# Three of a seven's six sums made in the accumulator banks, with a new order of products and of the attention stage

## The chip, the core and the metric

The kernel runs on one core of one Trainium2 chip. The metric is the device time of one execution in microseconds (us); lower is better. TensorE (PE) does the matmuls, VectorE (DVE), ScalarE (ACT) and GpSimd (POOL) the elementwise work, SyncE (SP) issues most of the DMAs. PE writes its results into eight accumulator banks, called `ps` in the rows, that DVE and ACT read.

## What is computed

```python
def _attn_ref(q, k, v):            # 4 batches x 8 heads x 576 positions x 64
    scores = np.matmul(q, k.transpose(0, 1, 3, 2)) / np.sqrt(D)
    scores = np.where(block_i >= block_j, scores, -1e9)   # causal in blocks of 64
    attn = softmax(scores)
    return np.matmul(attn, v)
def _moe_ref(x, w_in, w_out, s, b):    # x 2304 x 512, w_in 512 x 2048, w_out 2048 x 512
    r = np.maximum(x @ w_in, 0.0)
    return (s * (r * r) + b) @ w_out
def _moe2_ref(x, w1, w2, w3, w_out):   # w1, w2, w3 512 x 768, w_out 768 x 512
    return np.maximum(np.maximum(x @ w1, x @ w2), x @ w3) @ w_out
# reference: attention, heads joined to 2304 x 512, then _moe_ref, then _moe2_ref
```

All of it is in float32. The kernel splits each operand into a high and a low half and makes three matmuls of each product (high by high, high by low, low by high).

## The kernel before

**Attention** takes sixteen pairs of heads, one after the other. For a pair PE makes the scores of nine units of up to 576 columns, DVE takes each unit's maximum (L516), ACT the exponential with the row sums (L520, an ACTIVATE and a short read of its accumulator), PE turns the results by transposes (L581), ACT copies the turned tiles from the banks to SBUF (L363, `other<-ps`), and PE multiplies them by the values. ACT also copies the pair's result into the array `xf` (L363, `xf<-ps`). While a pair is worked on, the next pair's keys and queries are split: POOL takes high halves (L359), DVE low halves (L368, 64x1152), and ACT or POOL two small tiles of 64x128 called `k0`. A weight that layer 1 needs is read by DMA as words of 64 bits and converted by DVE, ACT, DVE, DVE (L704, L708, L712, L716), then split into halves. Three such weights are prepared from the twelfth pair on (`pre`).

**Layer 1, first half of its hidden units**: five chunks of tokens, eight blocks of 128 hidden units each (40 steps), with plain products of 128x512 or 128x384. Beside it DVE and ACT prepare the weights of what follows ("aside") and write them to DRAM (`wscr`, `bscr`): for layer 1's second half from step 8 on, for layer 2 from step 24 on in every other step, and then one in each seven of layer 1.

**Layer 1, second half, and layer 2's first three products** are made by "sevens": a product of 2x2 blocks by seven block products instead of eight (39 sevens: 12 in layer 1, 27 in layer 2). The seven products are named after the weight blocks: A11, S1, S2, S3, A12, S4, A22. Each is six matmuls of 128x384 into one bank. Four results C11, C12, C21, C22 come from seven products by sums. In the kernel before, each product has a bank of its own. ACT copies the first (L914), and DVE makes six sums in each seven (L902), each of a bank and an SBUF tile. In layer 1 ACT then makes relu, square and affine of the four results (`hidden`, L1232, L1237, L1244). In layer 2 DVE takes the maximum over the three weights (L1303). The blocks are fetched from `bscr` by `next_b`, seven for each seven, into a ring of eight places. Between the products of a seven stand the products with the second weight (`l2_half`, `l4`) of the seven before.

**What sets the order.** The functions only record operations with their reads and writes. `Sched.run` (L200) then goes through them with a cost for each engine and a latency for each pair of engines: at each step the engine that is free first takes the operation that is ready and stands earliest in the record, shifted by its kind's entry in `CFG["off"]`. An operation that may run on two engines takes the one that gets to it first (`CFG["pe"]`, `CFG["je"]`, `CFG["eng"]`). The order in which an engine gets its instructions is fixed when the program is built; on the chip an instruction whose input is late holds up all behind it on its engine. Banks are given out by `Banks.get`, the one that was taken longest ago first. A seven has four banks, the accumulators of the second product the other four.

Of the kernel before, what the change touches and what calls it, by code (L numbers as in the profile page):

```python
# [46 lines left out]
ABLK = ("A11", "S1", "S2", "S3", "A12", "S4", "A22")  # L47
BBLK = ("B11", "T1", "T2", "T3", "B21", "B22", "T4")
# [23 lines left out]
def c_act(n):  # L72
    return n / 1.2 + 51
# [199 lines left out]
def tile_attention_moe(ctx: ExitStack, tc: tile.TileContext, qk, vp, w_in, w_out, s_, b_, w123, w_out2, out):  # L273
# [96 lines left out]
    def mm(o, l, r, start, stop):  # L370
        nc.tensor.matmul(o, l, r, start=start, stop=stop)  # L371
# [376 lines left out]
    def prepare_b(key, kind):  # L748

        G, G2 = (convert(src, kind) for src in wsrc[key])  # L750
# [134 lines left out]
    def product(A, B, where):  # L885

        W, bank = wuse.pop(A), banks.get(where)
        o = bank.ap[:, 0:HN]
        for i in range(2):
            X = xs[B, i]  # L890

            def f(e, i=i, X=X):
                kk = slice(128 * i, 128 * i + 128)
                mm(o, W.ap[:, 0, kk], X.ap[:, 0, :], i == 0, False)
                mm(o, W.ap[:, 0, kk], X.ap[:, 1, :], False, False)
                mm(o, W.ap[:, 1, kk], X.ap[:, 0, :], False, i == 1)
            op("PE", 3 * c_mm(HN), f, reads=[(W, 0), (W, 1), (X, 0), (X, 1)], writes=[bank], kind="l1")
        return bank
# [5 lines left out]

    def seven(key, P1, dst, between):


        m1, u2, u3, u4 = (rings["u"].get() for _ in range(4))
        for a in ABLK:
            wuse[a] = ready.pop(key + (a,))  # L910
        M = product("A11", "B11", P1)

        def f(e, M=M):
            nc.scalar.activation(out=m1.ap, in_=M.ap[:, 0:HN], func=AF.Copy)  # L914
        op("ACT", c_act(HN), f, reads=[M], writes=[m1], kind="u")
# [4 lines left out]
        c = {"C22": dst("C22")}  # L920
        add_to(c["C22"], M5, u3)
        for _ in range(4):
            next_b()
        between()
        for x, a, b, u in (("C11", "A12", "B21", m1), ("C12", "S4", "B22", u4), ("C21", "A22", "T4", u3)):
            M = product(a, b, P1)
            c[x] = dst(x)
            add_to(c[x], M, u)
            next_b()
        return c  # L930
# [200 lines left out]
    def prepare_aside(todo_, kind):  # L1131
        if todo_:
            key = todo_.pop(0)
            (prepare_v if isinstance(key[0], str) else prepare_b)(key, kind)
# [73 lines left out]
    for i, (n_, f_) in enumerate(steps):  # L1208
        s_now, c = PASSES[n_]
        while direct and (("in", min(i + 2, HF - 1)) not in ready or i + 2 >= LAG and ("out", min(i + 2 - LAG, HF - 1)) not in ready):  # L1210
            prepare_direct("w")
        l1(c, f_, banks.get(SETS[0]))
# [223 lines left out]
```

## Time and profile before

| | |
|---|---|
| median of 3 runs | 845.12 us (844.29 to 845.18) |
| profiled execution | 843.48 us |
| its span, first to last instruction | 841.7 us |
| PE busy | 826.4 us (98%) |
| DVE busy | 644.5 us (77%) |
| ACT busy | 466.7 us (55%) |
| POOL busy | 47.5 us (6%) |
| mean granted TensorE clock | 0.997 of full speed |

Busy is the time in which an engine had at least one instruction under way. Matmuls overlap in their pipeline, so a busy PE is not always at its full rate; the count of matmuls in a stretch shows the rate. A group of rows below gives an instruction's line, engine, operation, output and input tile, shape, count, busy time and mean duration, then the idle time of its engine before it and who ended that.

### The profile page before, as it was taken

The page shows a single profiled execution, that of the slowest core. Times are in us where ns is not written, and L with a number is a line of the kernel's source. Part 1 is how long each engine was busy: PE and PEld are TensorE (multiplying, and loading weights), DVE is VectorE, ACT ScalarE, POOL GpSimd, SP SyncE. Part 2 cuts the span into 40 slices and gives each one's busy share as a digit, 9 for nine tenths or more (in the row PEclk, how much of TensorE's full clock was granted, in tenths as well). Part 3 has the DMA queues.
Part 4 walks back from the last instruction along what each step waited for, and adds up shares of the span by engine and source line. Part 5 has one row for each costly group of instructions (what it writes and reads, how often), then busy time and mean ns, then how long its engine had stood idle before and what let it go on. Part 6 is the DMA issues. An engine that isn't in the chain of part 4 may idle for free.

```text
span 841.7 us, 14337 instructions
## 1 busy us (share of the span) xinstructions
PE 826.4 (98%) x4922; PEld 749.0 (89%) x4922; DVE 644.5 (77%) x1329; ACT 466.7 (55%) x1077; POOL 47.5 (6%) x65
## 2 busy tenths in 40 slices
PE   8999999999999999999999999999999999999997
PEld 7777777778888889998999999999998999999996
DVE  7778889999879697895997865857569466937762
ACT  5889999998668577666857726721014111411112
POOL 6222222100000000000000000000000000000000
PEclk9999999999999999999999999999999999999999
DMA  7669777766878787999659526557665676557742
GB/s 278 178 197 267 211 238 238 226 209 205 307 264 292 262 282 281 332 367 365 218 186 365 167 96 210 154 182 251 203 206 162 219 219 213 175 178 229 230 126 76
DMA packets 86088, 190.82 MB, mean 227 GB/s; under 512 B 10240, under 2 KB 16640, under 8 KB 86016
## 3 DMA queue, kind: packets, MB, share of 16 engines
q1 hardware_dynamic: 85456, 189.38, 68.6%
q8 instruction: 39, 0.64, 0.3%
q10 hardware_dynamic: 560, 0.52, 0.2%
q14 instruction: 33, 0.27, 0.1%
HBM read 145.49 MB, written 40.71 MB: 221 GB/s over the span
## 4 chain that ended last, share of the span: by engine, by line
PE 74%; DVE 9%; DMA 7%; ACT 6%; issue 3%; POOL 0%; SPq 0%; ACTq 0%; DVEq 0%; POOLq 0%
PE ps L371 70%; DMA bscr<-other 5%; PE ps L581 4%; ACT other L520 2%; DVE other L716 2%; DVE arena L368 2%; ACT other L363 2%; DVE other L368 1%; DVE other L764 1%; DVE other L704 1%; DMA arena<-bscr 1%; DMA pscr<-other 1%; ACT other L708 1%; DVE other L712 1%; DMA arena<-arena 1%
## 5 line engine op out<-in xcount | busy, mean ns | idle before, releaser
L371 PE MATMUL ps<-arena 128*128 128x384 f32 (+6 forms) x3878 | 736.7, 348 | 5.5 <-ACT other L363 1.4
L371 PEld LDWEIGHTS ps<-arena 128*128 128x128 f32 (+1 forms) x3878 | 677.1, 189 | 59.2 <-ACT other L520 9.5
L902 DVE TENSOR_TENSOR other<-ps,other 128x384 f32<-128x384 f32 x273 | 145.9, 553 | 81.1 <-PE ps L371 77.9
L368 DVE TENSOR_TENSOR arena<-other,arena 128x384 fp32r<-128x384 f32 (+3 forms) x204 | 136.3, 682 | 20.7 <-ACT arena L355 17.7
L355 ACT ACTIVATE arena<-other 128x384 fp32r<-128x384 f32 (+3 forms) x124 | 66.1, 545 | 113.9 <-DVE other L1303 68.0
L363 ACT ACTIVATE other<-ps 128x512 f32<-128x512 f32 (+1 forms) x137 | 72.1, 581 | 33.3 <-PE ps L371 23.9
L516 DVE TENSOR_REDUCE other<-ps 128x1 f32<-128x448 f32 (+4 forms) x144 | 68.8, 513 | 21.1 <-PE ps L371 17.6
L520 ACT ACTIVATE other<-ps,other 128x448 f32<-128x448 f32 (+4 forms) x144 | 79.3, 564 | 9.1 <-DVE other L516 8.1
L914 ACT ACTIVATE other<-ps 128x384 f32<-128x384 f32 x39 | 19.1, 489 | 109.8 <-PE ps L371 89.4
L581 PE MATMUL ps<-ident,other 128*128 128x128 f32 x400 | 55.8, 280 | 4.4 <-ACT other L520 3.8
L371 PE MATMUL ps<-other 128*64 128x64 f32 (+5 forms) x640 | 54.9, 313 | 0.1
L355 ACT ACTIVATE other<-other 128x256 fp32r<-128x256 f32 (+2 forms) x87 | 37.0, 437 | 27.7 <-DMA bscr<-other 14.1
L368 DVE TENSOR_TENSOR other<-other 128x256 fp32r<-128x256 f32 (+1 forms) x105 | 46.0, 453 | 8.0 <-ACT other L355 7.4
L581 PEld LDWEIGHTS ps<-ident,other 128*128 128x128 f32 x400 | 45.0, 143 | 8.0 <-ACT other L520 5.2
L708 ACT ACTIVATE other<-other 128x512 f32<-128x512 f32 x56 | 38.2, 694 | 20.8 <-DVE other L704 20.7
L371 PEld LDWEIGHTS ps<-other 128*64 128x64 f32 (+1 forms) x640 | 29.7, 136 | 19.3 <-issue 14.3
L716 DVE SCALAR_TENSOR_TENSOR other<-other 128x512 uint32<-128x512 uint32 x56 | 38.3, 688 | 3.9 <-ACT other L708 2.9
L1232 ACT ACTIVATE other<-other 128x384 f32<-128x384 f32 x48 | 24.6, 517 | 29.2 <-DVE other L902 29.2
L1303 DVE TENSOR_TENSOR other<-other 128x384 f32<-128x384 f32 x72 | 38.7, 554 | 1.3
L359 POOL TENSOR_SCALAR arena<-other 128x1152 fp32r<-128x1152 f32 (+4 forms) x31 | 33.7, 1102 | 53.3 <-PE ps L371 42.6
L357 DVE TENSOR_SCALAR arena<-other 128x384 fp32r<-128x384 f32 (+2 forms) x73 | 27.8, 384 | 10.9 <-ACT other L962 6.9
L1244 ACT ACTIVATE other<-other,cst 128x384 f32<-128x384 f32 x48 | 32.7, 699 | 0.4
(38 smaller groups left out, 383.9 us busy)
## 6 DMA issues: line engine op xcount, KB each, us to landing
arena<-bscr SPq DMA_DIRECT2D x273, 256.0 KB, 3.1
bscr<-other SPq DMA_DIRECT2D x91, 256.0 KB, 3.7
other<-qk SPq DMA_DIRECT2D x30, 576.0 KB, 6.4
other<-w_out SPq DMA_DIRECT2D x22, 512.0 KB, 6.0
other<-w SPq DMA_DIRECT2D x18, 512.0 KB, 5.4
other<-vp SPq DMA_DIRECT2D x16, 544.0 KB, 5.0
other<-w_in SPq DMA_DIRECT2D x16, 512.0 KB, 4.2
wscr<-other SPq DMA_DIRECT2D x14, 512.0 KB, 5.8
```

Of the source, the lines that this page charges most:

```text
L355: nc.scalar.activation(out=dst, in_=src, func=AF.Copy, scale=m)
L359: nc.gpsimd.tensor_scalar(out=dst, in0=src, scalar1=m, scalar2=1.0, op0=ALU.mult, op1=ALU.mult)
L363: nc.scalar.activation(out=dst, in_=src, func=AF.Copy)
L368: eng[e].tensor_tensor(out=dst, in0=a, in1=b, op=ALU.subtract)
L371: nc.tensor.matmul(o, l, r, start=start, stop=stop)
L516: nc.vector.tensor_reduce(out=NM.ap[:, u:u + 1], in_=v, axis=AX.X if n <= 512 else AX.XY, op=ALU.max, negate=True)
L520: nc.scalar.activation(out=ev, in_=v, func=AF.Exp, bias=NM.ap[:, u:u + 1], scale=1.0, accum_out=DEN.ap[:, d:d + 1])
L581: nc.tensor.transpose(TB.ap[:, 128 * i:128 * i + 128], x, ident)
L708: nc.scalar.activation(out=hi_f, in_=hi_f, func=AF.Prelu, scale=W_REBIAS, alpha=W_SIGN)
L716: nc.vector.scalar_tensor_tensor(out=lo_w, in0=hi_w, scalar=3, in1=lo_w, op0=ALU.logical_shift_left, op1=ALU.bitwise_or)
L902: nc.vector.tensor_tensor(out=out_.ap, in0=bank.ap[:, 0:HN], in1=u.ap, op=ALU.add)
L1303: eng[e].tensor_tensor(out=u.ap, in0=c.ap, in1=u.ap, op=ALU.max)
```

## The change

The sums that need one operand in a bank are made by PE where it can: after ACT has copied a bank out, a later product is accumulated on it. For that the order of the seven products changes to A11, S1, A12, S2, S4, S3, A22. A11 and S1 open banks a and b. A12 opens a third, d. S2 is added on bank a after ACT has copied it (`m1`), S4 on bank b after ACT has copied that (`m5`), S3 on bank a after ACT has copied it again (`u2`). A22 is added on bank a after DVE has read it for C22, and the bank then holds C21, which nobody copies by itself: ACT's relu reads it in layer 1, DVE's maximum in layer 2. So a seven has three copies by ACT (line 907 of the changed kernel) and three sums by DVE (line 902) in place of one and six. Bank a now stays taken from the first product of a seven to the last.

```diff
-ABLK = ("A11", "S1", "S2", "S3", "A12", "S4", "A22")
-BBLK = ("B11", "T1", "T2", "T3", "B21", "B22", "T4")
+ABLK = ("A11", "S1", "A12", "S2", "S4", "S3", "A22")
+BBLK = ("B11", "T1", "B21", "T2", "B22", "T3", "T4")
...
-    def product(A, B, where):
-        W, bank = wuse.pop(A), banks.get(where)
+    def product(A, B, bank, start=True):
+        W = wuse.pop(A)
...
-                mm(o, W.ap[:, 0, kk], X.ap[:, 0, :], i == 0, False)
+                on = dict(skip_group_check=not start)
+                mm(o, W.ap[:, 0, kk], X.ap[:, 0, :], start and i == 0, False, **on)
...
+    def out_of(bank, u, func=AF.Copy, kind="u"):
+        def f(e):
+            nc.scalar.activation(out=u.ap, in_=bank.ap[:, 0:HN], func=func)
...
     def seven(key, P1, dst, between):
-        M = product("A11", "B11", P1)
-            nc.scalar.activation(out=m1.ap, in_=M.ap[:, 0:HN], func=AF.Copy)
-        M5 = product("S1", "T1", P1)
-        add_to(u2, product("S2", "T2", P1), m1)
-        add_to(u4, M5, u2)
-        add_to(u3, product("S3", "T3", P1), u2)
-        add_to(c["C22"], M5, u3)
...
+        a = banks.get(P1)
+        product("A11", "B11", a)
+        m1 = out_of(a, rings["u"].get())
+        b = banks.get(P1)
+        product("S1", "T1", b)
+        m5 = out_of(b, rings["u"].get())
+        d = banks.get(P1)
+        product("A12", "B21", d)
+        add_to(c["C11"], d, m1)
+        product("S2", "T2", a, False)
+        u2 = out_of(a, rings["u"].get())
+        product("S4", "B22", b, False)
+        add_to(c["C12"], b, u2)
+        product("S3", "T3", a, False)
+        add_to(c["C22"], a, m5)
         between()
+        product("A22", "T4", a, False)
+        c["C21"] = a
...
-            prepare_aside(aside, "w2")
-        if i >= CFG["aside2"] and i % 2:
-            prepare_aside(aside2, "w2")
+            prepare_aside(aside, "w2", gate)
+        if i in CFG["aside2"]:
+            prepare_aside(aside2, "w2", gate)
...
-CFG = {'aside': 8, 'aside2': 24,
+CFG = {'aside': 8,
+        'aside2': (16, 18, 20, 22, 24, 26, 28, 30),
...
-        'je': ['ACT'],
+        'je': ['ACT', 'DVE'],
...
-        'pe': ['ACT'],
+        'pe': ['ACT', 'DVE'],
...
-        'pre': (0, 0, 0, 0, 0, 0, 0, 0, 0, 0, 0, 1, 1, 1),
+        'pre': (0, 0, 0, 0, 0, 0, 0, 0, 1, 0, 0, 0, 0, 0, 0, 1, 0),
```

Five more things change. The copies of the turned tiles and of the results into `xf` may go to DVE as well as to ACT. The `k0` tiles of pairs after the second go to POOL alone, and of the low halves POOL may take some. The record's order inside a pair (`CFG["order"]`) and nearly all of the shifts in `CFG["off"]` are other numbers. Two weights of layer 1 are prepared during attention, at the ninth and the sixteenth pair, instead of three from the twelfth on. The eight preparations for layer 2 that stood in steps 25 to 39 stand in steps 16 to 30, and a preparation's loads now wait for the first product of their step or seven (`gate`).

On PE, where two sevens of layer 2 meet, every six matmuls are a block product. `Activation` and `DVE` are those engines' semaphores, the DMA names those of the block's fetch. Before, these are S3, A12, A22, S4 of one seven and A11 of the next:

```order
L371 MATMUL ps<-arena 128x384 [waits DMAHW5_49]
L371 MATMUL ps<-arena 128x384 x5
L371 MATMUL ps<-arena 128x384 [waits DMAHW6_49,Activation_49]
L371 MATMUL ps<-arena 128x384 x5
L371 MATMUL ps<-arena 128x384 [waits DMAHW1_49,DVE_49]
L371 MATMUL ps<-arena 128x384 x5
L371 MATMUL ps<-arena 128x384 [waits DMAHW7_49,DVE_49]
L371 MATMUL ps<-arena 128x384 x5
L371 MATMUL ps<-arena 128x384 [waits DMAHW0_49]
L371 MATMUL ps<-arena 128x384 x5
```

Now, at the same place, A12, S1, S2, S4 and S3 of one seven, in this order on PE:

```order
L371 MATMUL ps<-arena 128x384 [waits DMAHW4_49]
L371 MATMUL ps<-arena 128x384 x5
L371 MATMUL ps<-arena 128x384 [waits DMAHW1_49,DVE_49]
L371 MATMUL ps<-arena 128x384 x5
L371 MATMUL ps<-arena 128x384 [waits DMAHW3_49,Activation_49]
L371 MATMUL ps<-arena 128x384 x5
L371 MATMUL ps<-arena 128x384 [waits DMAHW5_49,Activation_49]
L371 MATMUL ps<-arena 128x384 x5
L371 MATMUL ps<-arena 128x384 [waits DMAHW6_49,Activation_49]
L371 MATMUL ps<-arena 128x384 x5
```

S1 waits until DVE has read the bank of the seven before, and S2, S4 and S3 each wait for a copy by ACT. Between the product whose bank is copied or read and the product that waits, there is one other product (six matmuls) here for S1, S4 and S3.

On ACT, in a middle pair of attention, before:

```order
L520 ACTIVATE other<-ps,other 128x448
L355 ACTIVATE other<-other 64x128
L520 ACTIVATE other<-ps,other 128x64
L363 ACTIVATE other<-ps 128x384
L520 ACTIVATE other<-ps,other 128x192
L363 ACTIVATE other<-ps 128x512
L520 ACTIVATE other<-ps,other 128x448
L520 ACTIVATE other<-ps,other 128x576
L520 ACTIVATE other<-ps,other 128x320
L363 ACTIVATE xf<-ps 128x64
L363 ACTIVATE xf<-ps 128x512
```

and now:

```order
L520 ACTIVATE other<-ps,other 128x192
L363 ACTIVATE other<-ps 128x512
L520 ACTIVATE other<-ps,other 128x64
L363 ACTIVATE other<-ps 128x384
L355 ACTIVATE arena<-xf 128x512
L363 ACTIVATE other<-ps 128x512
L520 ACTIVATE other<-ps,other 128x576
L363 ACTIVATE xf<-ps 128x64
L520 ACTIVATE other<-ps,other 128x448
L520 ACTIVATE other<-ps,other 128x320
L363 ACTIVATE other<-ps 128x384
```

The `k0` tile (64x128) is gone from ACT, and no large copy into `xf` stands between these exponentials; the exponentials are the same ones in another order.

## Rows read from the trace of the kernel before

**Rows 1.** Engines by stretch: start:end, length, busy (count) by engine, clock, DMA share, GB/s.

```profile
24.40:155.70 131.30, 127.88 (x1111) 96.60 (x1110) 110.46 (x170) 121.17 (x374) 33.05 (x40) 1.00 0.77 227
155.70:176.50 20.80, 19.54 (x189) 14.55 (x187) 18.77 (x42) 20.62 (x58) 0.00 (x0) 1.00 0.57 181
176.50:300.00 123.50, 123.50 (x551) 102.31 (x548) 109.11 (x254) 90.05 (x162) 0.00 (x0) 1.00 0.75 258
300.00:325.00 25.00, 24.53 (x128) 22.35 (x126) 22.37 (x56) 18.31 (x36) 0.00 (x0) 1.00 0.90 336
...
375.00:400.00 25.00, 23.16 (x131) 22.27 (x130) 14.40 (x30) 14.17 (x29) 0.00 (x0) 1.00 0.99 371
400.00:550.00 150.00, 150.00 (x866) 149.69 (x865) 122.58 (x280) 99.58 (x207) 0.00 (x0) 1.00 0.61 199
550.00:825.00 275.00, 275.00 (x1498) 263.71 (x1497) 181.80 (x359) 50.35 (x100) 0.00 (x0) 1.00 0.62 197
...
sum 841.70, PE 826.41 PEld 748.95 DVE 644.52 ACT 466.71 POOL 47.48; mean PE 82.64 PEld 74.90 DVE 64.45 ACT 46.67 POOL 4.75
```

**Rows 2.** Chain that ended last: the same seven transposes, thirteen pairs apart (start, length).

```profile
24.45 0.77 PE ps L581 x7
...
155.70 0.78 PE ps L581 x7
```

**Rows 3.** Engines by stretch, as Rows 1: two single pairs of attention.

```profile
85.95:95.39 9.44, 9.44 (x87) 7.41 (x86) 8.43 (x12) 9.00 (x29) 2.88 (x3) 1.00 0.59 194
95.39:106.21 10.82, 10.23 (x89) 7.39 (x87) 9.05 (x17) 9.93 (x34) 2.45 (x3) 1.00 0.78 225
```

**Rows 4.** Groups of instructions by shape, 0 to 176.5 us (attention): ACT, DVE and POOL.

```profile
L363 ACT ACTIVATE other<-ps 128x512 f32<-128x512 f32 x64 | 39.1, 631 | 2.4 <-PE ps L581 2.4
...
L363 ACT ACTIVATE other<-ps 128x384 f32<-128x384 f32 x48 | 23.9, 519 | 4.0 <-PE ps L581 3.9
...
L363 ACT ACTIVATE xf<-ps 128x512 f32<-128x512 f32 x15 | 9.3, 622 | 0.0
...
L355 ACT ACTIVATE other<-other 64x128 f32<-64x128 f32 x16 | 4.9, 309 | 0.4 <-DMA other<-qk 0.4
...
L363 ACT ACTIVATE xf<-ps 128x64 f32<-128x64 f32 x15 | 3.5, 237 | 0.0
...
L368 DVE TENSOR_TENSOR arena<-other,arena 64x1152 fp32r<-64x1152 f32 x14 | 28.6, 2045 | 1.5 <-POOL arena L359 1.3
...
L359 POOL TENSOR_SCALAR other<-other 64x128 f32<-64x128 f32 x16 | 4.8, 301 | 48.5 <-DVE other L516 21.0 <-PE ps L371 11.6 <-issue 8.8
```

**Rows 5.** Groups by shape, whole run: sums and weight conversion, DVE's copies, ACT's copy.

```profile
L902 DVE TENSOR_TENSOR other<-ps,other 128x384 f32<-128x384 f32 x273 | 145.9, 553 | 81.1 <-PE ps L371 77.9
...
L716 DVE SCALAR_TENSOR_TENSOR other<-other 128x512 uint32<-128x512 uint32 x56 | 38.3, 688 | 3.9 <-ACT other L708 2.9
L712 DVE TENSOR_SCALAR other<-other 128x512 uint32<-128x512 uint32 x56 | 23.5, 421 | 0.0
L704 DVE TENSOR_SCALAR other<-other 128x512 f32<-128x512 f32 x56 | 23.4, 420 | 2.7 <-DMA other<-w 2.2 <-DMA other<-w_out 0.5
...
L365 DVE COPY other<-ps 128x512 f32<-128x512 f32 x9 | 6.1, 683 | 14.5 <-DMA out<-other 14.5
...
L914 ACT ACTIVATE other<-ps 128x384 f32<-128x384 f32 x39 | 19.1, 489 | 109.8 <-PE ps L371 89.4 <-DVE other L902 20.4
```

**Rows 6.** Timeline at 383 to 388 us, DVE and PE (start, length, idle before and releaser).

```profile
383.72 0.36 DVE L357 TENSOR_SCALAR arena<-other 128x384 fp32r<-128x384 f32 x1 [0.46 <-ACT other L1244]
...
384.14 2.27 PE L371 MATMUL ps<-arena 128*128 128x384 f32 x9 [0.42 <-DVE arena L357]
...
387.67 2.54 PE L371 MATMUL ps<-arena 128*128 128x384 f32 x13 [1.27 <-DMA arena<-bscr]
```

**Rows 7.** Chain that ended last, at the end: from PE's last matmul to ACT.

```profile
799.94 35.29 PE ps L371 x179
...
835.30 0.61 ACT other L363
```

**Rows 8.** Groups by shape, 400 to 825 us: PE's matmuls of the sevens.

```profile
L371 PE MATMUL ps<-arena 128*128 128x384 f32 x2088 | 365.2, 334 | 0.0
```

More of the change, by code (lines that the diff above doesn't have):

```diff
@@ L368, in sub_to, with mm @@
         eng[e].tensor_tensor(out=dst, in0=a, in1=b, op=ALU.subtract)
-    def mm(o, l, r, start, stop):
-        nc.tensor.matmul(o, l, r, start=start, stop=stop)
+    def mm(o, l, r, start, stop, **k):
+        nc.tensor.matmul(o, l, r, start=start, stop=stop, **k)
     def load(size, f, eng="SP", after=(), lat=2000, **k):
@@ L746, in prepare_v, with prepare_b @@
         pair_out("wv", G.ap[..., 0], [(G, "lo")], 512, wscr[VAT_[key]], key, kind)
-    def prepare_b(key, kind):
-        G, G2 = (convert(src, kind) for src in wsrc[key])
+    def prepare_b(key, kind, after=()):
+        G, G2 = (convert(src, kind, after) for src in wsrc[key])
         half = slice(0, 256), slice(256, 512)
@@ L1129, in prepare_direct, with prepare_aside @@
             ready[key] = prepare_v(key, kind, key[0][0] + "w%d" % key[1], after)
-    def prepare_aside(todo_, kind):
+    def prepare_aside(todo_, kind, after=()):
         if todo_:
             key = todo_.pop(0)
-            (prepare_v if isinstance(key[0], str) else prepare_b)(key, kind)
+            (prepare_v if isinstance(key[0], str) else prepare_b)(key, kind, after=after)
     def next_b():
@@ L1228, in tile_attention_moe, with hidden @@
         ready["out", f_] = fetch("oc%d" % i, ("out", f_), kind="wf")
-    def hidden(u):
+    def hidden(u, bank=None):
         def f(e):
             nc.scalar.activation(out=u.ap, in_=u.ap, func=AF.Relu)
-        op("ACT", c_acts(HN), f, reads=[u], writes=[u], kind="h", lock=True)
+        if bank:
+            out_of(bank, u, AF.Relu, "h")
+        else:
+            op("ACT", c_acts(HN), f, reads=[u], writes=[u], kind="h", lock=True)
         def f(e):
@@ L1259, in dst @@
                 return rings["rc" if x[2] == "1" else "kp"].get()
+            gate = [len(sch.ops)]
             c = seven((i, "in"), P1, dst, between)
             f1, f2 = HF + i, HF + i + HF // 2
-            for x in ("C11", "C21", "C22", "C12"):
-                hidden(c[x])
+            bank, c["C21"] = c["C21"], dst("C21")
+            for x in ("C11", "C12", "C22", "C21"):
+                hidden(c[x], bank if x == "C21" else None)
             split_h((f1, 0), c["C11"])
@@ L1300, in tile_attention_moe, with f @@
                 c = seven((i, w), P1, dst, between)
-                for x in ("C22", "C11", "C12", "C21") if w else ():
-                    def f(e, u=best[x], c=c[x]):
-                        eng[e].tensor_tensor(out=u.ap, in0=c.ap, in1=u.ap, op=ALU.max)
-                    op(CFG_E("max", DVE=c_dve(HN), Pool=c_pooltt(HN)), 0, f, reads=[c[x], best[x]], writes=[best[x]], kind="h", lock=True)
+                if not w:
+                    out_of(c["C21"], dst("C21"))
+                for x in ("C11", "C12", "C22", "C21") if w else ():
+                    v = c[x].ap[:, 0:HN]
+                    def f(e, u=best[x], v=v):
+                        eng[e].tensor_tensor(out=u.ap, in0=v, in1=u.ap, op=ALU.max)
+                    op("DVE", c_dve(HN), f, reads=[c[x], best[x]], writes=[best[x]], kind="h", lock=x != "C21")
             split_h((i, 0), best["C11"])
@@ L1334 @@
                'hlo': ['DVE'],
-               'max': ['DVE'],
                'whi': ['ACT', 'DVE'],
@@ L1362 @@
                 'u': -200,
-                'w0': 250,
+                'w0': -975,
                 'w2': 100,
@@ L1376 @@
         'q0': ['ACT', 'SP'],
+        'q2d': 2,
         'raw': 4,
@@ L1380 @@
         'warm': 60,
-        'xs': 12}
+        'xs': 16}
 def kernel(**inputs):
```

58 lines of the change are left out of this document (28 added, 30 removed).

## The prediction

> **What bounds the kernel now.** I read the table of engines by stretch first, then the chain that ended last, then the groups by shape in attention, then the few places where PE waits after attention. The table [rows 1] has two regimes. From 176.5 us on PE is busy all the time but for 0.47 us in 300 to 325, 1.84 us in 375 to 400, and the tail. The counts say that this is the full rate: 866 matmuls of 384 columns in 150 us is 0.173 us each, the same wherever PE is full. The change leaves the number and the shapes of PE's matmuls as they are, so in that part it can win back only those stalls, however much it takes off DVE. In 550 to 825 us, DVE is busy 181.8 of 275 us and ACT 50.4, beside a full PE.
>
> Before 176.5 us it is different. In 24.4 to 155.7 us ACT is busy 121.2 of 131.3 us (92%), DVE 110.5 (84%), and PE has 3.4 us without any matmul. The chain passes the same seven transposes at 24.45 and 155.70 us, thirteen pairs apart [rows 2]: 131.25 / 13 = 10.10 us for a pair. A pair in which PE never stops takes 9.44 us; a slow one takes 10.82, and there ACT is busy 9.93 and DVE 9.05 us [rows 3]. So a pair has 0.66 us that is not PE's own, on the average, and thirteen have 8.5 us. In the last stretch, 155.7 to 176.5, ACT is the full engine: 20.62 of 20.80 us [rows 1].
>
> **The change, part by part.**
>
> *Attention: work leaves ACT.* Counted in the built order up to the last exponential, ACT loses 5 copies of 128x512 and 9 of 128x384 out of the banks, 8 large and 11 small copies into `xf`, and 14 `k0` tiles: 5 x 0.631 + 9 x 0.519 + 8 x 0.622 + 11 x 0.237 + 14 x 0.309 = 19.7 us [rows 4], of some 142 us that it is busy in 24.4 to 176.5. DVE gets the copies. A copy of 128x512 takes it 0.683 us [rows 5]; at ACT's durations for the rest that is about 5 x 0.68 + 9 x 0.52 + 8 x 0.68 + 11 x 0.24 = 16.1 us. Three weight conversions fewer begin there, 3 x (0.420 + 0.421 + 0.688) = 4.6 us [rows 5]. Net, DVE has 11.5 us more: its 110.5 + 18.8 us become 141 of 152 us, 93% (some of it falls into the first pair). POOL has 14 tiles of 0.301 us more [rows 4], and is mostly idle. So ACT goes from 93% to (141.8 - 19.7) / 152 = 80%, and DVE comes to stand where ACT stood. PE's order in a pair keeps its form: two blocks of matmuls by the values, and transposes between scores. The most to win is 8.5 us (every pair at 9.44). The other end is a loss: were DVE to set the pairs as ACT does in the slow one, the 11.5 us would come on top. I take half of the 8.5, 4.2 us, since a shorter queue on ACT shortens every exponential's wait while DVE still has its heavy pairs. In the last stretch PE has 1.26 us idle beside a full ACT [rows 1]; I take 1.0. For the first pair, whose splitting is dealt out anew, I take 0, between -1.5 and +1.5. Sum: -5.2 us.
>
> *Shared port.* DVE's subtraction of 64x1152, with both inputs in SBUF, takes 2.045 us [rows 4]; an estimate by its columns from the copy of 128x512 (0.683, [rows 5]) is 1.5. It runs where POOL works on the next pair's high halves. The Trainium skill (SBUF — State Buffer, "SBUF: two separate sides") gives a reason: a VectorE operation with two SBUF inputs and a GpSimd operation share a port pair that one holds for its whole instruction while the other blocks. The trace agrees in kind. By that rule the 14 added tiles on POOL could hold DVE up 14 x 0.301 = 4.2 us at most. The sum would be 841.5 by it if all of that stood on PE's path, between the forecast and the third rival; without it the sum stands as it is.
>
> *Sevens: sums move from DVE to PE's banks.* DVE loses 156 sums of 0.553 us (86 us), ACT gets 78 copies of 0.489 us and nine more for layer 2's first results [rows 5]. On a full PE that is worth 0 by itself. It costs where a copy is late. Now three products in each seven wait for a copy or a read, and in the built order 96 waits (66 on ACT, 30 on DVE) have one other product between the product that fills the bank and the one that waits. That product is 6 x 0.173 = 1.04 us. Against it stand: the last matmul's record runs 0.334 us [rows 8], 0.16 beyond its slot; 0.07 from PE's end to ACT's start (835.23 to 835.30) [rows 7]; the copy, 0.49, or the sum, 0.55; and 0.06 back to PE (384.08 to 384.14) [rows 6]. Together 0.78 on ACT and 0.84 on DVE, so 0.26 and 0.20 us are left. In layer 2 ACT is busy 50 of 275 us and the copy meets an empty queue: 0. In layer 1 ACT is at 66% [rows 1], and its queue holds relu, square and affine of 0.5 to 0.7 us. A copy that finds one just begun is late by up to 0.7 - 0.26 = 0.44 us, and PE and the products behind it wait. Ends: 0, and 12 sevens x 3 x 0.44 = 15.8 us. I take 1.0, near the lower end, as the order was laid out so that most copies find ACT free.
>
> *Preparations for layer 2 come earlier.* In 375 to 400 us PE makes 131 matmuls, 144.5 at its full rate (25 / 0.173): 2.3 us lost. One part is 1.27 us for a block from `bscr` while the DMA engines are 99% busy [rows 1, 6]; another is a split by DVE that waited for ACT's affine, 0.42 us [rows 6]. Eight preparations, each two loads of 512 KB (one for an output weight) with its conversions and up to seven stores of 256 KB through SP's queue, go from steps 25 to 39 to steps 16 to 30, some 45 us earlier, where no block is fetched yet. DMA was at 75% there, so the stores fit, and SP's queue is freer when the sevens start fetching. I take 2.0 of the 2.3 us; ends 0 and 2.8 (with the 0.47 in 300 to 325).
>
> *Layer 1's weights start later.* Three conversions that were done in attention fall into its first steps: with the low halves' subtraction, at about 0.69, 3 x 2.2 = 6.6 us of DVE, and each step takes two weights after the third. In the first three steps only one is due, so they hide there; 0, with the other end at 6.6 us. *The tail* has the same last products and stores: 0.
>
> Sum: 843.48 - 5.2 + 1.0 - 2.0 = 837.3 us for an execution like the profiled one. The median of the runs shown lies 845.12 - 843.48 = 1.64 us higher, so I forecast 838.9.
>
> **The rivals.**
>
> First, attention keeps its pairs. The waits before PE's transposes are still for exponentials, which stay on ACT; if that latency, not ACT's load, makes the 0.66 us, nothing is won there. For it: pairs of 10.82 us have ACT idle for 0.9 us. Against it: the fast pairs have less work on ACT and DVE. It gives 838.9 + 5.2 = 844.1.
>
> Second, the other side: copies are late in the sevens of layer 1. The price is up to 15.8 us in place of 1.0, 853.7. The whole gain of 5.2 + 2.0 us is gone when the 36 waits lose 7.2 / 36 = 0.20 us each. For it: there is 0.26 us where the kernel before, counted the same way, left 0.5 us and more; ACT's queue is in order. Against it: the low load in two thirds of the sevens.
>
> Third, DVE takes ACT's place: its load of 93% in attention, its subtractions of 2.045 us beside POOL [rows 4], and the late weights hold back what ACT frees. Then some 5 of the 7.2 us come back: 844. Heavy pairs speak for it (DVE 9.05 of 10.82, [rows 3]), the light ones (8.43 of 9.44) leave 1 us.
>
> **How the numbers follow.** Forecast 0.53, first rival 0.15, second 0.14, third 0.18. The forecast's own range is 833 to 842.5. From these, faster by over 0.2% (1.7 us; about what a measurement tells from no change), below 843.4: nearly all of the forecast and a third of the first and third, 0.64. Within 0.2%: 0.19. Slower: 0.17, most of the second and the ends of the others. For 8 in 10 the range goes from 832 to 848: all of what attention and the stalls could give, less the forecast's own doubt, up to half of the second rival's price.
>
> **What would show it.** In the profile after: a pair near 9.7 us and ACT's busy share in attention near 80%, DVE's over 90%; PE without idle time at 383 to 388 us; matmuls at 0.173 us through layer 2's sevens. Wrong would be: pairs still at 10.1 us; PE idle released by ACT's line 907 in the sevens, by over 0.2 us at a time; fewer than 144 matmuls in 25 us between 400 and 550; PE waiting for weights in the first steps of layer 1.

## The result, and the profile after

The changed kernel takes 834.61 us (median of 4 runs, 833.58 to 835.5) against 845.15 for the kernel before (4 runs, 844.29 to 845.28): a ratio of 0.9871 [0.9854, 0.9889], 10.5 us less. The forecast was 838.9 us, 6.2 less. The profiled execution takes 834.42 us, its span 832.6.

To see where the 9.06 us between the two profiled executions went, I cut both spans at three points that PE passes in either: the first large block by the values of the first pair (first matmul), the same block thirteen pairs later, and the last transposes.

| stretch | before | after | change | forecast |
|---|---|---|---|---|
| start to the first block | 22.32 | 19.12 | -3.20 | 0 |
| thirteen pairs | 131.25 | 127.06 | -4.19 | -4.2 |
| from there to the last transposes | 19.85 | 18.58 | -1.27 | -1.0 |
| last transposes to the end | 668.26 | 667.88 | -0.38 | -1.0 |

The first two rows hide what is steady and what is not. Up to the second pair's large block, eight of the experiments below have the same order of instructions as after, yet that block starts at 29.14 us in after and anywhere from 29.16 to 31.83 us in the eight; in before it starts at 32.52 us. The twelve pairs from there on take 121.05 us in before (120.96 and 121.01 in two experiments with its order) and 117.04 in after (116.78 to 116.90 in seven experiments with its order). So the -4.0 us of these twelve pairs and the -1.27 us of the last stretch are firm, 5.3 us together. The -3.4 us ahead of them are not: of the nine profiles, after's has the earliest start of that block.

Engines by stretch of after (columns as in [rows 1]), the thirteen pairs cut at the transposes that [rows 2] show for before, then the last stretch and three later ones:

```profile
21.04:148.10 127.06, 125.02 (x1113) 97.28 (x1109) 120.34 (x198) 111.78 (x337) 42.84 (x52) 1.00 0.80 231
148.10:168.90 20.80, 20.80 (x205) 16.67 (x202) 20.69 (x47) 19.43 (x52) 0.00 (x0) 1.00 0.61 184
375.00:400.00 25.00, 24.44 (x139) 23.57 (x138) 15.97 (x35) 20.59 (x41) 0.00 (x0) 1.00 1.01 354
400.00:550.00 150.00, 149.37 (x858) 148.34 (x857) 108.95 (x256) 98.32 (x201) 0.00 (x0) 1.00 0.64 212
550.00:825.00 275.00, 275.00 (x1483) 261.57 (x1483) 132.19 (x256) 71.32 (x145) 0.00 (x0) 1.00 0.62 193
```

A pair now takes 127.06 / 13 = 9.77 us in place of 10.10. ACT's share fell from 92 to 88%, DVE's rose from 84 to 95%: DVE is now the fuller engine. In 375 to 400 us PE makes 139 matmuls in place of 131, but in 400 to 550 it makes 858 in place of 866: what was won in the one stall came back in others. 858 in 150 us is 143 in 25 us, just below the 144 that the prediction named as a sign of being wrong. In 550 to 825 DVE has lost 50 us of work, and the end does not move for it.

What PE waits for after attention, in before and then in after (waited for, us, times, longest):

```profile
PE ps L371 <- DMA arena<-bscr: 1.3, 1, 1.3
PE ps L371 <- DVE arena L357: 0.4, 1, 0.4
PE ps L371 <- ACT other L363: 0.4, 1, 0.4
```

```profile
PE ps L371 <- DMA arena<-bscr: 0.9, 2, 0.4
PE ps L371 <- DVE arena L368: 0.9, 1, 0.9
PE ps L371 <- DVE other L902: 0.2, 1, 0.2
```

No wait in after ends on an ACT copy (L907). The 0.9 on L368 is new: at 188 us a weight of layer 1 is prepared late, another of the prediction's signs of being wrong.

Two single pairs of after, one of the two slow ones that are left (the other takes 10.81) and a fast one:

```profile
76.79:87.81 11.02, 10.16 (x87) 7.53 (x86) 10.93 (x19) 9.51 (x29) 4.08 (x4) 1.00 0.87 252
97.46:106.73 9.27, 9.27 (x87) 7.40 (x86) 8.94 (x15) 8.27 (x25) 2.71 (x4) 1.00 0.82 250
```

The fast pair is faster than the 9.44 us that I took for the floor [rows 3]; in the slow one DVE is busy 10.93 of 11.02 us, so it has no time left there.

The first pair, 16 to 20 us, before and then after; the column behind the five engines is the granted clock:

```profile
16.00:18.00 2.00, 1.09 (x5) 0.85 (x6) 1.94 (x4) 1.94 (x8) 1.77 (x3) 0.70 0.79 309
18.00:20.00 2.00, 2.00 (x12) 2.00 (x11) 2.00 (x2) 1.44 (x3) 0.80 (x1) 0.50 0.63 130
```

```profile
16.00:18.00 2.00, 2.00 (x17) 1.93 (x18) 0.46 (x2) 2.00 (x6) 1.52 (x3) 1.00 0.99 361
18.00:20.00 2.00, 2.00 (x12) 1.27 (x13) 2.00 (x4) 0.90 (x4) 2.00 (x2) 1.00 0.70 274
```

The first transposes on PE with the wait ahead of them, before and then after:

```profile
16.43 0.44 PE L581 MATMUL ps<-ident,other 128*128 128x128 f32 x2 [1.28 <-ACT other L520]
```

```profile
15.15 0.44 PE L581 MATMUL ps<-ident,other 128*128 128x128 f32 x2 [1.04 <-ACT other L520]
```

Before has 0.50 of the clock (1.2 GHz) there, after PE had waited 1.28 us ahead of the first transposes; after waits 1.04 us at that place and keeps 2.4 GHz. I had not looked at this stretch.

### The profile page after: what moved, and what is told of

Its sections match the earlier page's. It is cut to its first block, busy times and chain, and to the rows that moved or that the text cites. A ratio compares the mean times of both kernels' runs of the same rounds, so it can differ in the third digit from the quotient of the medians.

```text
span 832.6 us, 14344 instructions
## 1 busy us (share of the span) xinstructions
PE 820.8 (99%) x4922; PEld 747.7 (90%) x4922; DVE 589.7 (71%) x1227; ACT 489.9 (59%) x1097; POOL 57.7 (7%) x78
## 4 chain that ended last, share of the span: by engine, by line
PE 84%; DVE 7%; DMA 6%; issue 1%; ACT 1%; POOL 0%; SPq 0%; DVEq 0%; ACTq 0%; POOLq 0%
PE ps L371 80%; PE ps L581 4%; DVE arena L368 2%; DMA other<-qk 1%; DMA other<-w_in 1%; DMA arena<-bscr 1%; DMA other<-w_out 1%; DVE other L716 1%; DVE other L516 1%; DMA arena<-wscr 1%; DMA bscr<-other 1%; DVE other L368 1%; DVE xf L812 0%; DVE other L712 0%; DVE other L764 0%
## 5 line engine op out<-in xcount | busy, mean ns | idle before, releaser
L371 PE MATMUL ps<-arena 128*128 128x384 f32 (+7 forms) x3878 | 731.1, 347 | 5.3 <-ACT other L520 1.5
L368 DVE TENSOR_TENSOR arena<-other,arena 128x384 fp32r<-128x384 f32 (+3 forms) x205 | 134.0, 665 | 30.3 <-ACT arena L355 25.3
L907 ACT ACTIVATE other<-ps 128x384 f32<-128x384 f32 x138 | 67.6, 490 | 147.6 <-PE ps L371 147.3
L902 DVE TENSOR_TENSOR other<-ps,other 128x384 f32<-128x384 f32 x117 | 64.9, 554 | 97.6 <-PE ps L371 94.6
L355 ACT ACTIVATE arena<-other 128x384 fp32r<-128x384 f32 (+4 forms) x115 | 63.0, 554 | 67.0 <-PE ps L371 54.0
L363 ACT ACTIVATE other<-ps 128x512 f32<-128x512 f32 (+1 forms) x122 | 63.8, 561 | 41.9 <-PE ps L371 30.0
L520 ACT ACTIVATE other<-ps,other 128x576 f32<-128x576 f32 (+4 forms) x144 | 78.2, 555 | 10.1 <-DVE other L516 9.0
L516 DVE TENSOR_REDUCE other<-ps 128x1 f32<-128x576 f32 (+4 forms) x144 | 68.4, 512 | 4.9 <-PE ps L371 3.2
L357 DVE TENSOR_SCALAR arena<-other 128x384 fp32r<-128x384 f32 (+1 forms) x82 | 30.4, 374 | 28.6 <-ACT other L1260 16.1
L368 DVE TENSOR_TENSOR other<-other 128x256 fp32r<-128x256 f32 (+1 forms) x105 | 46.9, 456 | 3.7 <-ACT other L355 3.1
L365 DVE COPY other<-ps 128x512 f32<-128x512 f32 (+2 forms) x29 | 17.6, 620 | 27.4 <-DMA out<-other 26.4
L368 DVE TENSOR_TENSOR arena<-xf,arena 128x384 fp32r<-128x384 f32 (+1 forms) x56 | 32.8, 598 | 1.3 <-ACT arena L355 1.0
```

What stands on the lines that cost most here:

```text
L355: nc.scalar.activation(out=dst, in_=src, func=AF.Copy, scale=m)
L363: nc.scalar.activation(out=dst, in_=src, func=AF.Copy)
L368: eng[e].tensor_tensor(out=dst, in0=a, in1=b, op=ALU.subtract)
L371: nc.tensor.matmul(o, l, r, start=start, stop=stop, **k)
L516: nc.vector.tensor_reduce(out=NM.ap[:, u:u + 1], in_=v, axis=AX.X if n <= 512 else AX.XY, op=ALU.max, negate=True)
L520: nc.scalar.activation(out=ev, in_=v, func=AF.Exp, bias=NM.ap[:, u:u + 1], scale=1.0, accum_out=DEN.ap[:, d:d + 1])
```

## The experiments

### Half of the change at a time

Attention's settings of after in the kernel before, with the sevens and the steps of the preparations as they were:

```diff
-CFG = {'aside': 8, 'aside2': 24, 'eng': {'k0': ['ACT', 'Pool'], ...
+CFG = {'aside': 8, 'aside2': 24, 'eng': {'k0': ['Pool'], ...   # all of after's, but for 'aside2' and 'ew'
```

> The kernel before with the changed kernel's settings of attention alone (record's order, shifts, engines of the splits and copies, when layer 1's weights are prepared); sevens and the preparations for layer 2 as before. Theory A (attention makes the gain; the sevens are worth about nothing on a full PE): the changed kernel is 10.5 us below before, of which its trace has 8.8 us by the start of layer 1, so 835 to 837.5, with the stalls of before at the start of the sevens (some 3 us) kept. Theory B (the lighter DVE in the sevens and the earlier preparations carry half or more of it): 840 or more.

Measured: 848.15 us (846.55 to 850.59), ratio 1.0043 [1.0028, 1.0058]. Attention has after's pace (last transposes at 165.64 us, after 164.76, before 173.42), yet the kernel is slower than before. The rest takes 683.1 us in place of 668.3. Most of it is at one place: PE's rows where layer 1's sevens start, and engines by stretch there:

```profile
384.73 5.12 PE L371 MATMUL ps<-arena 128*128 128x384 f32 x27
396.54 6.67 PE L371 MATMUL ps<-arena 128*128 128x384 f32 x25 [6.69 <-DMA arena<-bscr]
```

```profile
389.86:396.54 6.68, 0.00 (x1) 0.03 (x1) 0.56 (x1) 1.81 (x4) 0.00 (x0) 0.83 1.04 401
396.54:401.10 4.56, 4.56 (x14) 4.56 (x15) 0.90 (x2) 1.54 (x3) 0.00 (x0) 0.50 0.70 229
```

A block that a seven needs comes 6.7 us late, and behind the wait PE runs at half clock: 14 matmuls in 4.56 us, 0.33 us each in place of 0.173. The profiled execution, 850.59 us, is the slowest of the eight, so the median loses some 2.4 us less than this profile. The gain in attention is real but can be lost whole 220 us later. The time lies in theory B's range, but neither theory had the kernel slower than before.

The other half, new sevens with their steps and gate, attention as before:

```diff
-        'je': ['ACT', 'DVE'], 'order': '2vbaAB4067p|1||c|5|...
+        'je': ['ACT'], 'order': '2ba40AB7c6v|15dCeDEp8|3'   # all of before's, but for 'aside2' and 'ew'
```

> The changed kernel with the settings of attention of before; the sums on the banks, the new order of products, and the earlier, gated preparations stay. Theory A: 844 to 846.5, about the time before: stalls of 4 us go and others of about the same size come. Theory B: 840 or less.

Measured: 851.52 us (849.09 to 854.49), ratio 1.0079 [1.0057, 1.01]. The pairs are those of before. In the profile the first block comes at 24.99 us, 2.7 us later than in before, with half clock from 17.73 to 24.56 us, though the order up to there is before's; the part after attention takes 5.2 us more, and there a copy is late once, with half clock behind it:

```profile
460.74 2.69 PE L371 MATMUL ps<-arena 128*128 128x384 f32 x9 [2.35 <-ACT other L907]
```

```profile
458.39:460.74 2.35, 0.00 (x0) 0.00 (x0) 1.35 (x5) 0.95 (x3) 0.00 (x0) 1.00 1.00 384
461.46:464.88 3.42, 3.42 (x13) 3.42 (x12) 2.06 (x5) 3.29 (x7) 0.00 (x0) 0.50 0.90 313
```

Either half alone loses by the medians; together they win 10.5 us.

### Which part of the rest holds the dense part together

To the first experiment's kernel I added the new steps for layer 2's preparations and the gate:

```diff
-        if i >= CFG["aside2"] and i % 2:
-            prepare_aside(aside2, "w2")
+        if i in CFG["aside2"]:          # (16, 18, ..., 30)
+            prepare_aside(aside2, "w2", gate)
```

> The kernel before with the changed kernel's attention settings, as in the first experiment, and now also with its steps for layer 2's preparations (16 to 30 in place of 25 to 39) and the gate on their loads. Sevens and their six sums on DVE are those of before. Theory T (what the first experiment lost in the sevens, 6.7 us in one wait for a fetch and some 10 us more of stalls and half clock behind it, came from preparation traffic in front of the fetches in SP's queue): the earlier steps take that traffic away; about 664 us of dense part and the attention of after, so 834 to 838 us. Theory S (the lighter DVE of the new sevens is what keeps the dense part full): the stalls stay though they may move, 842 to 849 us.

And from the changed kernel I took them away (the same lines the other way round):

> The changed kernel with the old steps for layer 2's preparations (every other step from 25 on) and without the gate. New sevens, new attention. Theory T: the traffic meets the first fetches of the sevens again, a wait of several us for a block at the start of the sevens, and half clock behind it: 842 to 850 us. Theory S: the lighter DVE makes up for it, 834.6 to 837 us. By my prediction's term for this part (2.0 us of stalls) 836.6 us.

Measured: 843.21 us (840.9 to 845.57), ratio 0.9982 [0.9968, 0.9995], and 842.94 us (839.98 to 843.91), ratio 0.9976 [0.9966, 0.9987]. Neither theory alone holds. With after's attention the four kernels are

| | old sevens | new sevens |
|---|---|---|
| old steps, no gate | 848.15 | 842.94 |
| new steps, gate | 843.21 | 834.61 |

so each of the two is worth 5 to 9 us, and both are needed. The four medians were not measured side by side, and before's own median was 844.20 to 845.15 us beside them, so the differences hold to about 1 us. Steps and gate were changed together and not tried apart. What PE waits for after attention, first with the old sevens and new steps, then with the new sevens and old steps:

```profile
PE ps L371 <- DMA arena<-bscr: 2.7, 2, 2.0
PE ps L371 <- DVE other L902: 2.6, 1, 2.6
```

```profile
PE ps L371 <- DMA arena<-bscr: 4.7, 2, 4.4
PE ps L371 <- ACT other L907: 0.9, 2, 0.5
```

With the old sevens a sum by DVE is 2.6 us late; with the old steps a block from `bscr` is 4.4 us late. After has neither.

### Is it the bytes that make the blocks late?

In the first experiment's kernel the loads of the preparations bring less:

```diff
-            nc.sync.dma_start(out=G.ap..., in_=src)
+            nc.sync.dma_start(out=G.ap...[0:8 if kind == "w2" else 128], in_=src[0:8 if kind == "w2" else 128])
```

> The kernel of the first experiment (before, with the changed kernel's attention settings; 848.15 us, with a wait of 6.7 us for a fetch at 389.5 us), every instruction kept, but the loads of the preparations beside layer 1 (from step 8 on) bring 8 of 128 partitions, 32 KB in place of 512 KB. Theory B (the bytes: the DMA engines are 90 to 100% busy between 300 and 400 us, and the preparations' loads and the sevens' fetches share them): the waits for blocks and weights go, the dense part loses 7 us or less in place of 21.9, 831 to 837 us. Theory Q (the order of waits in SP's queue: a load or store that waits holds up the fetches behind it): the waits stay, 844 to 848 us.

Measured: 839.73 us (837.18 to 841.7), ratio 0.9935 [0.9915, 0.9954]; 8.4 us less than the first experiment, between the two theories and nearer to B. DMA issues of the first experiment at 380 to 400 us (KB each, median us to landing), and its DMA engines (the bytes and the share):

```profile
q1 hardware_dynamic: 3680, 7.45, 98.7%
...
arena<-bscr SPq DMA_DIRECT2D x11, 256.0 KB, 6.1
```

and PE's waits with the small loads:

```profile
PE ps L371 <- DMA arena<-bscr: 3.1, 1, 3.1
PE ps L371 <- DVE arena L368: 0.6, 2, 0.5
PE ps L371 <- DVE arena L357: 0.5, 1, 0.5
```

The DMA engines were full for 20 us (7.45 MB), and with fewer bytes more than half of the loss goes. Full engines alone do not tell the kernels apart: in the same 20 us they are busy 98.1% in before (7.19 MB) and 98.9% in after (6.88 MB), and no block is later than 1.3 us there. A wait of 3.1 us stays at the same place. The late fetch in the chain that ended last, with the whole loads and then with the small ones:

```profile
389.54 6.87 DMA arena<-bscr
```

```profile
382.66 3.98 DMA arena<-bscr
```

PE stops at 389.85 and at 383.71 us. So the fetch takes 2.9 us less with fewer bytes, and what stays is that it goes out only 0.3 and 1.1 us before PE needs the block. What holds it back in SP's queue was not measured by itself.

### Is it ACT's load that made the pairs slow?

The changed kernel, its order kept, with the copies that it gave to DVE put back on ACT. In the trace they are 37, 16 of turned tiles and 21 into `xf`; the 33 of the expectation leave out the end of the stage.

```diff
-                copy_to(e, PT.ap[:, o], TB.ap[:, 0:n])
+                copy_to("ACT", PT.ap[:, o], TB.ap[:, 0:n])
-                copy_to(e, xf[:, hp, t0 + tok:t0 + tok + n], O.ap[:, src])
+                copy_to("ACT", xf[:, hp, t0 + tok:t0 + tok + n], O.ap[:, src])
```

> The changed kernel with its order kept word for word, except that the 33 copies that DVE makes in attention (14 of turned tiles, 19 into xf) are issued on ACT at the same place in the order. ACT's load theory (a shorter queue on ACT is what made the pairs faster): some 16 us are back on ACT, its busy share in attention goes from 88% to near 100%, and most of the 5.5 us that the pairs gained is lost: 838.5 to 841. Order theory (the new order of a pair and the shifts made it, ACT has room): 834 to 836.

Measured: 839.83 us (839.24 to 840.5), ratio 0.9943 [0.9927, 0.9958], 5.2 us more than after. Its thirteen pairs, then the twelve behind the first of them in this kernel, in before and in after:

```profile
18.71:150.40 131.69, 127.39 (x1109) 97.33 (x1108) 112.30 (x171) 119.45 (x366) 43.69 (x56) 1.00 0.78 226
```

```profile
31.16:150.40 119.24, 116.98 (x1024) 89.80 (x1023) 101.59 (x156) 109.72 (x336) 36.71 (x48) 1.00 0.79 227
```

```profile
32.52:153.57 121.05, 118.64 (x1029) 89.47 (x1026) 101.62 (x157) 112.60 (x348) 30.88 (x38) 1.00 0.77 230
```

```profile
29.14:146.18 117.04, 115.15 (x1025) 89.70 (x1024) 110.79 (x184) 102.65 (x310) 37.96 (x48) 1.00 0.80 231
```

The 131.69 looks like before's 131.25 again, but 12.45 us of it are the first of the thirteen pairs, where kernels with after's order differ by over 2 us from profile to profile (9.28 to 11.59 us). In the steady twelve, 2.2 of the 4.0 us go with the copies back on ACT. In the last stretch all of the gain goes: 20.12 us here, 19.85 in before, 18.58 in after. So the copies' move off ACT makes 3.7 of the 5.3 us of the two. The other 1.5 us come from the rest of attention's settings, with ACT still the fullest engine but PE (109.72 of 119.24 us, 92%): the order inside a pair, twelve of the 22 shifts (not nearly all, as the list of changes has it), the engines of the `k0` tiles and of the splits, and the weights prepared at other pairs. None of these was tried alone, nor was an order laid out for copies on ACT. The first block is at 18.71 us, ahead of any copy by DVE, so the first pair's gain is not the copies'.

### How much room has a copy in a seven?

Each of a seven's copies by ACT done twice, then, in another run, followed by a read of 32 columns only:

```diff
+            for _ in range(2 if kind == "u" else 1):
                 nc.scalar.activation(out=u.ap, in_=bank.ap[:, 0:HN], func=func)
```

> The changed kernel with each copy out of a seven's bank made twice by ACT (the second writes the same again), its order kept: each copy ends some 0.4 to 0.5 us later. If the room of 0.26 us that was worked out for the waits with one product between is right: 66 such waits are late by 0.12 to 0.23 us each, 8 to 15 us, 842 to 850, most of it in layer 2 where the copies meet an empty queue now. If PE has more room than that: 834 to 837.

```diff
             nc.scalar.activation(out=u.ap, in_=bank.ap[:, 0:HN], func=func)
+            if kind == "u":
+                nc.scalar.activation(out=u.ap[:, 0:32], in_=bank.ap[:, 0:32], func=func)
```

> The changed kernel with its order kept; after each copy of a seven's bank ACT reads the first 32 columns of the same bank once more into the same tile, which puts about 0.2 us between the copy and PE (the 128x64 copy took 0.237 us). In the run with a second whole copy each late wait cost 0.33 us: 0.23 us of lateness and 0.10 us in which the next matmul was slow too. If that means a room of 0.26 us as worked out in the prediction, layer 2 loses nothing now: 834.6 to 837 us, a few late waits in layer 1. If the room is 0.1 us or less, some 66 waits lose 0.1 us of lateness and 0.1 us of restart each: 845 to 849 us.

Measured: 857.36 us (856.52 to 858.0), ratio 1.015 [1.0131, 1.0169], and 839.64 us (837.7 to 839.87), ratio 0.9931 [0.9917, 0.9946]. The first lost more than either theory had it; the second lies between its two cases. What PE's weight loads wait for in 550 to 825 us with the whole second copy; then, with the short read, ACT's groups by shape in that stretch (count, busy us, mean ns) and engines by stretch:

```profile
PEld ps L371 <- ACT other L908: 14.8, 35, 1.1
```

```profile
L907 ACT ACTIVATE other<-ps 128x384 f32<-128x384 f32 x90 | 44.3, 492 | 111.3 <-PE ps L371 111.3
L909 ACT ACTIVATE other<-ps 128x32 f32<-128x32 f32 x90 | 17.8, 198 | 2.9
```

```profile
550.00:825.00 275.00, 275.00 (x1477) 258.40 (x1476) 132.20 (x256) 88.86 (x235) 0.00 (x0) 1.00 0.63 195
```

What PE waits for ends later than in after by 0.52 us in the first run (the two copies start 0.52 us apart) and by 0.23 us in the second (0.198 for the read and 0.03 before it). In the trace 33 of layer 2's waits lose about 0.33 us each in the first (the first matmul starts 0.23 us late, the one behind it 0.10 more), and 34 lose 0.04 us in the second. 0.52 - 0.33 and 0.23 - 0.04 both give 0.19 us: that is the room, in place of the 0.26 that I worked out. In after no matmul of layer 2's sevens starts late: these waits are met with 0.19 us to spare. Behind the expectation for the short read I had split the 0.33 into 0.23 of lateness and 0.10 of a restart; that would give a room of 0.29 in the first run and 0.19 in the second, so the two agree only if the whole 0.33 counts as lateness.

### What is left in attention

The multiplications by the reciprocal (L812) on POOL in place of DVE, and then left out, the order kept in both:

```diff
-                eng[e].tensor_tensor(out=src, in0=src, in1=N.ap[:, 0:n], op=ALU.mult)
+                nc.gpsimd.tensor_tensor(out=src, in0=src, in1=N.ap[:, 0:n], op=ALU.mult)
```

> The changed kernel with the order of all other instructions kept; the multiplications by the softmax's reciprocal (line 812, 128x512, 0.69 us without disturbance) run on POOL in place of DVE. In the two slow pairs that are left (11.02 and 10.81 us) DVE is 99 and 97% busy and PE 92%. Theory D (DVE's load is what is left of attention's loss): each of the two pairs loses about 1.2 us, 831.5 to 833.5 us. Theory P (two inputs from SBUF on POOL and DVE's operations keep each other waiting, and POOL takes twice DVE's time for one): DVE's work beside it stretches by what it was relieved of, and layer 1's inputs come later: 835 to 843 us.

```diff
-                eng[e].tensor_tensor(out=src, in0=src, in1=N.ap[:, 0:n], op=ALU.mult)
+                pass
```

> The changed kernel with the order of all other instructions kept; the 20 multiplications by the softmax's reciprocal (line 812, 0.69 to 0.81 us each on DVE, 11 of them between 24 and 168 us) are left out. When they were moved to POOL the pair of 11.02 us came down to 9.63, but three others went up to 10.55 to 11.53. Theory D (the third rival's remainder: DVE is what makes the two slow pairs of 11.02 and 10.81 us): both come down to about 9.6 us, and nothing else goes up: 2.6 us less, 831 to 833 us. Theory E (the slow pairs wait for something else, an exponential or a split): they stay above 10.5, 833.5 to 835 us.

Measured: 839.28 us (836.16 to 843.24), ratio 0.9932 [0.9909, 0.9955], and 832.02 us (829.47 to 833.29), ratio 0.9839 [0.9817, 0.986]. On POOL, by engines, the pair that had taken 11.02 us, one that had been fast (9.65 us) and the one that had taken 10.81, and POOL's group:

```profile
79.56:89.19 9.63, 9.63 (x86) 7.46 (x86) 9.21 (x16) 8.96 (x29) 4.93 (x5) 1.00 0.92 266
89.19:99.74 10.55, 9.78 (x87) 7.55 (x86) 10.29 (x18) 9.05 (x28) 4.14 (x5) 1.00 0.78 239
109.01:120.54 11.53, 10.11 (x87) 7.49 (x86) 10.53 (x18) 9.25 (x29) 5.30 (x5) 1.00 0.75 213
```

```profile
L812 POOL TENSOR_TENSOR xf<-xf,other 128x512 f32<-128x512 f32 x11 | 15.5, 1415 | 10.5 <-DMA other<-scr 10.5
```

The first comes down as theory D has it, the others go up: POOL takes 1.415 us for one multiplication and stands 10.5 us before them waiting for their reciprocals' DMA, with the next pair's high halves behind it in its queue. The twelve pairs take 118.27 us, 1.2 more than in after. Most of the rest of this run's loss in the profile, 2.7 us, is there before the second pair's block, with half clock from 15.65 to 22.48 us, where this edit changes nothing; so the 4.7 us of the medians are not the price of the move alone. Left out, the two slow pairs:

```profile
76.80:86.30 9.50, 9.50 (x87) 7.42 (x85) 9.08 (x17) 8.89 (x29) 3.68 (x4) 1.00 0.90 249
105.18:115.50 10.32, 10.00 (x87) 7.49 (x86) 9.37 (x18) 9.38 (x29) 3.65 (x4) 1.00 0.84 233
```

Attention ends 2.4 us sooner (162.38 for 164.76). The first slow pair was DVE's load; the second comes down by 0.5 us only, so something else holds it; what, was not looked for.

### The first pair

Filler matmuls in PE's gaps of the first pair, in before and in after:

```diff
-        'warm': 60,
+        'warm': 80,
```

> The kernel before, with 20 more filler matmuls (128x256, results unused) in PE's gaps of the first pair, 7 of them between the last scores and the first transposes; nothing else moves. In the profiled execution of before PE waits 1.28 us ahead of the first transposes (16.43 us) and the granted clock is 0.5 from 16.80 to 20.21 us; in after PE waits 1.04 us there and the clock stays. Theory C (a part of the first pair's 3.2 us is the half clock after that idle time, not the new order): with the gap filled the clock stays at 1.00, 20.21 - 16.80 = 3.41 us at half clock saves up to 1.7 us; 842.5 to 844 us, and granted clocks of 0.999 and more. Theory O (the order of the first pair sets it, the clock is hidden behind its splits): 844 to 846 us.

```diff
-        'warm': 60,
+        'warm': 74,
```

> The changed kernel with 14 more filler matmuls in the first pair's gaps; there the planner then takes a few of the first pair's transposes and scores in another order, behind it all is as in the changed kernel. Its runs so far gave mean granted clocks of 0.997 to 0.999 and 833.58 to 835.5 us. Theory C: all runs have 0.999 or more and the time is at the lower end, 833 to 834.3 us. Theory O, or fillers that make the transposes wait: 834.5 to 837 us.

Measured: 845.08 us (842.67 to 848.77), ratio 1.0003 [0.9986, 1.002], and 836.15 us (835.26 to 838.12), ratio 0.9893 [0.9875, 0.9911]. The filled kernel before, 16 to 18 us:

```profile
16.00:18.00 2.00, 1.53 (x13) 1.17 (x12) 1.94 (x4) 2.00 (x8) 1.79 (x3) 1.00 0.75 292
```

In this profile the clock stays at 1.00 and the first block comes at 21.15 us in place of 22.32. So 1.2 of the 3.2 us fits the half clock, and 2.0 (21.15 to 19.12) the new order. The medians do not show the 1.2: no gain that can be told, though the three of twelve runs with a mean clock of 0.999 or more took 842.67 to 844.34 us, below the median. In the profiles with after's attention order the first block comes at 18.7 to 19.7 us in eight, and at 21.9 to 22.6 in three, two of them at half clock before it. By the second pair's block some of that is made up (29.14 to 31.83 us, as said above). How much of the 3.2 us a median run has is left open; after's profile is at the lucky end. The filled after is no better than after: its first transposes start at 17.09 us in place of 15.15.

## Why the prediction was right, and where its sizes were off

The direction, the place and the two terms of attention held: pairs -4.2 forecast, -4.19 measured; last stretch -1.0 and -1.27; and the copies on ACT are shown as the cause of the larger part, 3.7 of the 5.3 us of the twelve pairs and the last stretch. That the pairs agree to 0.01 us is luck: the half that I took of 8.5 us was a guess, and 0.2 of the -4.19 lies in the first of the thirteen pairs, which differs by more than that from profile to profile. The reasoning on ACT was partly luck, too. I put it at 80% by taking 19.7 us of row durations off its busy time. ACT's records overlap: its groups in before's thirteen pairs sum to 162 us where it is busy 121. The groups lost 17.7 us and the busy time 9.4, so ACT stands at 88%. DVE at 95% is close to the 93% forecast.

The step that failed is "for the first pair, whose splitting is dealt out anew, I take 0, between -1.5 and +1.5": it measured -3.20. I never looked at before's first 24 us, where a wait of PE and a stretch at half clock could be read. It is more than the whole of the 2.9 us between -6.2 and -9.06 in the profiled executions; the last stretch adds 0.3, and the dense part takes 0.6 back. 1.2 of the 3.2 us fit the half clock in before; the other 2.0 came with the new order, in a profile that starts early for that order.

The dense part: "late copies +1.0" measured 0 on ACT and 0.2 on DVE, with a room of 0.19 us in place of 0.26 and 0.20. "Earlier preparations -2.0" and "weights later 0" did not add up as separate terms. The weights cost 0.9 (L368). The preparations' steps are worth 8.3 us in the new kernel (842.94 to 834.61), not 2.0: I read their price from stalls of a kernel whose attention ended 8.7 us later. The stalls that went (1.84 us at 375 to 400) came back elsewhere, and the sum is -0.38.

The last 1.5 us of the 10.5 are in the medians: before's lies 1.67 us above its profiled execution, after's 0.19, and I had added 1.64 for after too.

The rivals. First (the pairs keep their pace): refuted by the pairs themselves, 121.05 to 117.04 us for twelve, and over half of that goes with the copies back on ACT. Second (late copies): not seen in after, but near; 0.23 us more per copy costs 5 us, 0.52 us more costs 22.7. Third (DVE in ACT's place): true of one of the two slow pairs, worth 2.4 us in attention and not the 5 forecast.

With the rule on the shared port (SBUF — State Buffer, "SBUF: two separate sides" in the Trainium skill) the trace agrees in kind: between 24 and 168 us POOL's 64x128 tiles take 0.444 us on the average in after, beside a fuller DVE, against 0.290 in before. But DVE's 64x1152 subtraction became shorter there, 1.742 us against 2.023, so the 4.2 us that I bounded it by did not come.

What stays open, beside the first pair and the 1.5 us of attention that the copies do not explain: why the old attention with the old sevens and steps fits its DMA traffic (2.1 us of waits after attention) while the new attention with the same sevens and steps does not (12.1 us). Every setting makes the planner lay out the order anew; that one term was not taken apart further.

## What to carry to other kernels

Look at the first microseconds and at the granted clock in them before a term there is set to zero. A profile of one execution can have its first microseconds at the lucky or the unlucky end: cut the span where several kernels with the same order agree. A gain in an early stage moves every transfer behind it: test it with the later stages as they are, and look at the fetches that go out late where the DMA engines are full, for there it can be lost whole. Room on a wait is best measured by adding two known delays behind the same producer: what each is late by gives the same room, or the model is wrong.

## What the runs showed of the hardware that was not expected

After PE stood idle for 6.69, 2.35 and 3.06 us (three kernels), the granted clock was 0.50 in a stretch behind it and matmuls of 384 columns started 0.32 us apart; after single waits of 0.9 us in after and of 1.27 us in before [rows 6] it stayed at 1.00. In the first experiment the half clock cost 4.56 - 14 x 0.173 = 2.1 us on top of the wait. So one late block is paid for twice. A product can be accumulated on a bank that ACT has copied out in the meantime without loss when one other product of six matmuls (1.04 us) stands between, with 0.19 us to spare.

With one and the same order of instructions the first 30 us differ by 2.7 us between nine profiles (29.14 to 31.83 us for the second pair's block), while the twelve pairs behind agree within 0.3 us (116.78 to 117.04 us in eight profiles).
